# A fused attention, gated MLP and top-2 expert kernel: the second batch's attention in steps of three, the third chunk from the third unit on

## The chip, the cores and the metric

The kernel runs on one core of one Trainium2 chip. The metric is device time in microseconds of one execution. Before the change it was 981.42 us (median of 3 runs, 981.08 to 982.90).

## The reference, cut to what matters

```python
# attention: B=4 batches, H=8 heads, S=576 tokens, D=64, M=32 memory slots
a = exp(phi - max(phi, axis=tokens)); a /= sum(a, axis=tokens)
k_m, v_m = a^T @ k, a^T @ v                      # per head, 32 x 64
attn = softmax((q @ k_m^T) / 8); x = attn @ v_m  # x: 2304 tokens x 512
# gated MLP, d_ff = 1536
x = (sigmoid(x @ w_gate) * (x @ w_val)) @ w_out
# top-2 of 8 experts, F = 1024, noisy router
logits = x @ g + log1p(exp(x @ n)) * noise
out[t] = sum over the two best e of weight_e * (relu(x[t] @ w1[e]) @ w2[e])
```

## The kernel before

The weights of the gated MLP come as 64-bit numbers, and x and the weights are each kept as a high and a low fp16 part, so that every product is three passes of matmuls. The part that the change touches is the front of the program: attention, rounding of the weights, and the first products of the MLP, which all run at once.

**Products.** `stage1(c, (f,))` (lines 410 to 437) makes the gate and value of one chunk c of 256 tokens and one slice f of 128 hidden columns. It is called a product here: 24 matmuls of 256 columns on TensorE into one of four `pg` buffers of PSUM, then tanh on ScalarE (L432), a multiplication on VectorE (L433), and the split of the result into `gT` high (ScalarE, L435) and low (VectorE, L436), which frees the buffer. The third chunk (tokens 512 to 767) lies across two batches, so its products have 48 matmuls, of 64 and 192 columns, and need the attention of the second batch. The first three chunks have 36 products, and all of these are made before the second product of the MLP (`stage2`, L448) begins. Products are numbered 1 to 36 here, in the order in which TensorE has them.

**Weights.** `weights()` (lines 327 to 373) is a generator. A job is one matrix part of 256 columns (gate or value of a unit u, 6 units), or 256 rows of the output matrix, and each comes in two halves, loaded by `wload` into four `w64` buffers on the queue of SyncE. A half is converted by ScalarE (L321), two integer operations of VectorE (L323, L324) and an addition on GpSimd (L325, which frees the buffer). Per job ScalarE sums squares (L359); per unit a small matmul (`norm2`, L82, tile `pmx`) turns two sums into a scale, and then the pair is split (ScalarE L376, VectorE L377). A product of unit u needs the split pair u. Of the output matrix nothing is needed before L448.

**Attention.** `attend(b)` (line 953) is a generator too: softmax of the features (`features`, L201 to L206), the memories (`memory`, L163 to L190, for each half of the heads: two transposes, 20 or 40 small matmuls L176, the copies L178 and L181, a transpose L186, the copies L190 into `kbd`), a scale (`values_scale`, L213 and a `pmx` matmul), then for three groups of tokens the scores (L233, L230), their softmax over VectorE, ScalarE and GpSimd (L237 to L246), a transpose (L254) with its copy (L256), the result (L271, L264) and its split into the high and low x (ScalarE L274, VectorE L275). All of its PSUM tiles (`pa`) come from the same four `pg` buffers.

**What sets the order.** `build` (lines 966 to 1001) writes the front down as a mixture: `turns` takes one step of each generator named. After every product of the first two chunks come three steps of the weights and, while the second batch isn't done, one of the attention. The framework then orders each engine's instructions itself, by their priority and by what it expects to be ready; attention has a raised priority (`AHEAD1`). In the built program every engine works through its list strictly in this order, and so does the load queue on SyncE.

Of the kernel before, what the change touches and what calls it, by code (L numbers as in the profile page):

```python
# [61 lines left out]
class Kern:  # L62
# [841 lines left out]
    def build(self):  # L904
# [28 lines left out]
        def ahead_by(n):  # L933
            return tc.high_priority(n) if n else ExitStack()
# [26 lines left out]
        def attentions():  # L961
            for b in range(B):
                yield from attend(b)

        def turns(*gs):

            for g in gs:
                with ahead_by(offset.get(g, 0)):
                    next(g, None)
                while self.wanted:  # L970
                    self.att_load(*self.wanted.pop(0))

        self.attended = self.tokens_ready = 0
        atts, weights = attentions(), self.weights()
# [7 lines left out]
        def first(c, f):  # L982
            while self.tokens_ready < (c + 1) * CH:
                turns(atts)
            self.stage1(c, (f,))
        for u in range(6):
            while self.wdone < 2 * u + 2:
                turns(weights)
            for c in range(2):
                for f in (2 * u, 2 * u + 1):  # L990
                    first(c, f)
                    turns(weights, weights, weights)
                    if self.attended < 2:
                        turns(atts)
            if u >= 3:
                for _ in range(2):
                    first(*next(third))
                    turns(weights, weights, weights)
        for c, f in third:
            first(c, f)  # L1000
            turns(weights, weights, weights)
# [104 lines left out]
```

## Time and profile before

| what | value |
|---|---|
| median of 3 runs | 981.42 us |
| profiled execution | 978.12 us |
| its span (first to last instruction) | 976.4 us |
| TensorE busy | 922.5 us, 94% |
| VectorE, ScalarE busy | 468.7 us, 468.4 us, 48% each |
| mean granted TensorE clock | 0.973 |

The 1.72 us between the span and the time of the profiled execution lie around the program. The share of busy time is an average over the whole program: VectorE is below half over all, and near nine tenths in the front.

### The profile page before, as it was taken

The page shows a single profiled execution, that of the slowest core. Times are in us where ns is not written, and L with a number is a line of the kernel's source. Part 1 is how long each engine was busy: PE and PEld are TensorE (multiplying, and loading weights), DVE is VectorE, ACT ScalarE, POOL GpSimd, SP SyncE. Part 2 cuts the span into 40 slices and gives each one's busy share as a digit, 9 for nine tenths or more (in the row PEclk, how much of TensorE's full clock was granted, in tenths as well). Part 3 has the DMA queues.
Part 4 walks back from the last instruction along what each step waited for, and adds up shares of the span by engine and source line. Part 5 has one row for each costly group of instructions (what it writes and reads, how often), then busy time and mean ns, then how long its engine had stood idle before and what let it go on. Part 6 is the DMA issues. An engine that isn't in the chain of part 4 may idle for free.

```text
span 976.4 us, 18894 instructions
## 1 busy us (share of the span) xinstructions
PE 922.5 (94%) x7547; PEld 641.1 (66%) x7547; DVE 468.7 (48%) x1285; ACT 468.4 (48%) x979; POOL 209.6 (21%) x211
## 2 busy tenths in 40 slices
PE   5668889999999999999999989999999999999995
PEld 4447679766678877877776547657474757565652
DVE  3889884234543454567542504635353545432110
ACT  4788684234425344546431416647364646553230
POOL 1553420001011001020102154032232323131102
PEclk8689899999999999999999999999999999999998
DMA  9678474033022006474516959556757676745303
GB/s 301 219 221 284 148 248 154 18 89 104 23 71 72 23 23 189 133 216 147 202 24 168 350 112 195 179 129 130 200 118 204 115 187 122 172 80 75 40 12 43
DMA packets 125898, 135.28 MB, mean 139 GB/s; under 512 B 71792, under 2 KB 88304, under 8 KB 125296
## 3 DMA queue, kind: packets, MB, share of 16 engines
q1 hardware_dynamic: 115824, 113.30, 40.0%
q0 software_dynamic: 9984, 20.75, 11.9%
q8 instruction: 60, 0.98, 0.4%
q14 instruction: 30, 0.25, 0.1%
HBM read 87.97 MB, written 30.86 MB: 122 GB/s over the span
## 4 chain that ended last, share of the span: by engine, by line
PE 86%; DVE 4%; DMA 4%; ACT 2%; POOL 1%; issue 1%; SPq 0%; POOLq 0%; DVEq 0%; ACTq 0%
PE pg L426 26%; PE ph L770 20%; PE py L784 19%; PE px L448 14%; PE pa L233 1%; PE pa L176 1%; DMA w<-wo 1%; DVE pw L323 1%; DMA xe<-xg 1%; DMA w<-wv 1%; PE pa L271 1%; DVE w L377 1%; PE pl L476 1%; PE pmx L82 0%; DVE w L324 0%
## 5 line engine op out<-in xcount | busy, mean ns | idle before, releaser
L426 PE MATMUL pg<-x,w 128*128 128x256 f16 (+3 forms) x3456 | 309.1, 249 | 9.1 <-ACT w L376 4.8
L426 PEld LDWEIGHTS <-w 128*128 128x128 f16 x3456 | 271.2, 100 | 41.8 <-issue 7.0
L784 PEld LDWEIGHTS <-hT 128*128 128x128 f16 (+1 forms) x960 | 100.0, 105 | 105.5 <-DVE hT L776 1.0
L448 PE MATMUL px<-wo,gT 128*128 128x512 f16 x648 | 146.8, 379 | 0.0
L790 POOL DMA_INDIRECT out<-y,mts x40 | 63.9, 1596 | 227.4 <-ACT y L789 226.2
L770 PE MATMUL ph<-xe,w1a 128*128 128x312 f16 (+2 forms) x768 | 104.7, 299 | 4.3 <-DMA xe<-xg 4.3
L448 PEld LDWEIGHTS <-gT 128*128 128x128 f16 x648 | 62.2, 98 | 66.8
L784 PE MATMUL py<-w2a,hT 128*128 128x512 f16 (+1 forms) x480 | 104.9, 379 | 0.6 <-DVE hT L776 0.6
L784 PE MATMUL py<-w2b,hT 128*128 128x512 f16 (+1 forms) x480 | 104.7, 379 | 0.0
L770 PE MATMUL ph<-xe,w1b 128*128 128x312 f16 x768 | 102.8, 296 | 0.0
L432 ACT ACTIVATE sg<-pg,gs 128x256 f32<-128x256 f32 (+3 forms) x144 | 56.2, 416 | 90.2 <-PE pg L426 88.6
L592 POOL DMA_INDIRECT meta<-mt,vi x36 | 36.2, 1006 | 292.1 <-DVE vi L589 169.8
L776 DVE TENSOR_TENSOR hT<-r,hT 128x312 f16<-128x312 f32 (+2 forms) x128 | 56.6, 479 | 83.5 <-ACT hT L775 82.9
L770 PEld LDWEIGHTS <-w1a 128*128 128x128 f16 x768 | 75.6, 99 | 31.8 <-DMA xe<-xg 4.8
L770 PEld LDWEIGHTS <-w1b 128*128 128x128 f16 x768 | 75.2, 98 | 26.8
L789 ACT ACTIVATE y<-py,css 128x512 f32<-128x512 f32 (+1 forms) x40 | 27.5, 687 | 128.0 <-PE py L784 123.5
L433 DVE SCALAR_TENSOR_TENSOR pg<-sg,pg 128x256 f32<-128x256 f32 x108 | 45.9, 425 | 87.6 <-ACT sg L432 87.4
L774 ACT ACTIVATE r<-ph 128x312 f32<-128x312 f32 (+2 forms) x128 | 49.0, 428 | 78.8 <-PE ph L770 72.7
L435 ACT ACTIVATE gT<-pg 128x256 f16<-128x256 f32 x108 | 41.0, 380 | 46.0 <-DVE pg L433 45.7
L755 POOL DMA_INDIRECT xg<-xs,mts x40 | 44.9, 1122 | 72.6 <-DMA xe<-xg 27.8
L436 DVE SCALAR_TENSOR_TENSOR gT<-pg,gT 128x256 f16<-128x256 f32 x108 | 45.4, 420 | 27.9 <-ACT gT L435 27.9
L775 ACT CAST hT<-r 128x312 f16<-128x312 f32 (+2 forms) x128 | 52.4, 460 | 0.4
(307 smaller groups left out, 870.5 us busy)
## 6 DMA issues: line engine op xcount, KB each, us to landing
wo<-w SPq DMA_DIRECT2D x48, 512.0 KB, 5.6
st<-kv SPq DMA_DIRECT2D x16, 512.0 KB, 5.2
f<-w SPq DMA_DIRECT2D x16, 512.0 KB, 6.2
wsp<-hl SPq DMA_DIRECT2D x16, 512.0 KB, 3.5
w<-wg SPq DMA_DIRECT2D x12, 512.0 KB, 5.0
w<-wv SPq DMA_DIRECT2D x12, 512.0 KB, 4.9
w<-wo SPq DMA_DIRECT2D x12, 512.0 KB, 4.0
out<-z SPq DMA_DIRECT2D x23, 256.0 KB, 3.0
```

The lines of the kernel that those rows point to most:

```text
L426: nc.tensor.matmul(pg[:, j, s:e], w[:, l, k, fo : fo + P], self.xT[b][r][:, k, t0 : t0 + e - s], start=n == 0, stop=n == 3 * KT - 1)
L432: nc.scalar.activation(sg[:, s:e], pg[:, 0, s:e], AF.Tanh, scale=self.gate_scale(b, u))
L433: nc.vector.scalar_tensor_tensor(pg[:, 1, :], sg, 1.0, pg[:, 1, :], op0=ALU.add, op1=ALU.mult)
L436: nc.vector.scalar_tensor_tensor(g[:, 1, :], pg[:, 1, :], 2.0 ** -16, g[:, 0, :], op0=ALU.mult, op1=ALU.subtract)
L448: nc.tensor.matmul(p, g[:, l, t * P : (t + 1) * P], self.wob[f // 2][:, r, f % 2, :], start=f + i == 0, stop=f == FT - 1 and i == 2)
L755: self.nc.gpsimd.indirect_dma_start(out=xg.rearrange("p a b -> p (a b)"), out_offset=None, in_=self.xs[:rows, :], in_offset=bass.IndirectO ...
L770: nc.tensor.matmul(p[:, : t1 - t0], w1[:, l, k, f * P : (f + 1) * P], xe[:, x, t0:t1], start=n == 0, stop=n == 3 * KT - 1)
L774: nc.scalar.activation(r, p[:, : t1 - t0], AF.Relu, scale=2.0 ** -19)
L775: nc.scalar.copy(self.hT[:, 0, f, t0:t1], r)
L776: nc.vector.tensor_sub(self.hT[:, 1, f, t0:t1], r, self.hT[:, 0, f, t0:t1])
L784: nc.tensor.matmul(py, self.hT[:, l, f, i * P : i * P + m], w2[:, w, f, :], start=n == 0, stop=n == 3 * F2T - 1)
L790: d = nc.gpsimd.indirect_dma_start(out=self.out, out_offset=bass.IndirectOffsetOnAxis(ap=mt[:m, 0:1], axis=0), in_=y[:m], in_offset=None, ...
```

## The change

In the loop over the six units, attention takes up to three steps, not one, after each product of the first two chunks. The products of the third chunk start in the loop with the third unit (u = 2) instead of the fourth, three for each unit instead of two, so that all twelve are taken in the loop; beside each of these the weights take two steps instead of three. What is computed, and how many instructions there are, stays the same.

```diff
@@ -990,12 +990,13 @@
                 for f in (2 * u, 2 * u + 1):
                     first(c, f)
                     turns(weights, weights, weights)
-                    if self.attended < 2:
-                        turns(atts)
-            if u >= 3:
-                for _ in range(2):
+                    for _ in range(3):
+                        if self.attended < 2:
+                            turns(atts)
+            if u >= 2:
+                for _ in range(3):
                     first(*next(third))
-                    turns(weights, weights, weights)
+                    turns(weights, weights)
         for c, f in third:
             first(c, f)
             turns(weights, weights, weights)
```

On TensorE, this stands in the list before the change where the fourth product ends (`pg_658`) and the fifth, the first of the second unit (`w2`), begins (`pg_707`):

```order
L426 MATMUL pg_658<-x0_289,w1_82 128x256
L82 MATMUL pmx_471<-wum_428,onef_64 128x2
L426 LDWEIGHTS w2_83
L426 MATMUL pg_707<-x0_289,w2_83 128x256
L426 LDWEIGHTS w2_83
L426 MATMUL pg_707<-x1_290,w2_83 128x256
```

And this stands there after it, from the end of the fourth product (`pg_747`) to the fifth (`pg_824`); `pa_805` and `pa_872` are the scores of the second batch, `pmx_694` the scale of the fourth pair of weights, `pmx_797` the scale of the second batch:

```order
L426 MATMUL pg_747<-x0_289,w1_82 128x256
L82 MATMUL pmx_471<-wum_428,onef_64 128x2
L176 MATMUL pa_720<-st_554,a_710 32x128 x2
L186 MATMUL pa_789<-idf_60,km_741 128x128
L233 MATMUL pa_805<-kbd0_125,st_661 128x64 x8
L82 MATMUL pmx_694<-wum_538,onef_64 128x2
L426 LDWEIGHTS w2_83
L426 MATMUL pg_824<-x0_289,w2_83 128x256
L426 LDWEIGHTS w2_83
L426 MATMUL pg_824<-x1_290,w2_83 128x256
L82 MATMUL pmx_797<-vm_793,onef_64 128x1
```

The memories and the first scores of the second batch, and two scales, now come ahead of the fifth product. Before, the scores stood at the twelfth and thirteenth product, and attention ended inside the twentieth; now it ends inside the seventh. Products of the third chunk stood from the 17th place on and now stand from the 13th on.

On VectorE, this stands in the list before the change from the end of the fourth product (its `gT_686`) to the end of the fifth (`gT_737`):

```order
L436 SCALAR_TENSOR_TENSOR gT_686<-pg_658,gT_686 128x256
L88 TENSOR_SCALAR w3s_644<-w3h_643 128x2
L89 TENSOR_SCALAR w3i_645<-w3h_643 128x2
L433 SCALAR_TENSOR_TENSOR pg_707<-sg_732,pg_707 128x256
L324 SCALAR_TENSOR_TENSOR w10_91<-w64_545,pw_741 128x512
L323 TENSOR_SCALAR pw_748<-w64_593 128x512
L377 SCALAR_TENSOR_TENSOR w6_87<-w7_88,w3s_644,w6_87 128x1024
L436 SCALAR_TENSOR_TENSOR gT_737<-pg_707,gT_737 128x256
```

And after it the same place begins so (the fourth product is `pg_747`; `smx` and `ex` belong to the second batch's softmax):

```order
L436 SCALAR_TENSOR_TENSOR gT_775<-pg_747,gT_775 128x256
L324 SCALAR_TENSOR_TENSOR w9_90<-w64_461,pw_611 128x512
L201 TENSOR_REDUCE pmx_1051<-phi_905 128x1
L323 TENSOR_SCALAR pw_781<-w64_536 128x512
L323 TENSOR_SCALAR pw_858<-w64_545 128x512
L87 TENSOR_SCALAR sv1h_799<-pmx_797 128x1
L237 TENSOR_REDUCE smx_814<-pa_805 128x16
L88 TENSOR_SCALAR sv1s_800<-sv1h_799 128x1
L89 TENSOR_SCALAR sv1i_801<-sv1h_799 128x1
L239 TENSOR_TENSOR ex_816<-pa_805,smx_814 128x512
L237 TENSOR_REDUCE smx_881<-pa_872 128x16
```

The softmax of the second batch now stands between the fourth and the fifth product, 27 instructions where there were 6.

## Rows read from the trace of the kernel before

**Rows 1.** The page's busy tenths in 40 slices of 24.4 us.
```profile
PE   5668889999999999999999989999999999999995
DVE  3889884234543454567542504635353545432110
PEclk8689899999999999999999999999999999999998
```

**Rows 2.** Stretches: length, busy PE, PEld, DVE, ACT, POOL; clock, DMA share, GB/s.
```profile
39.20:62.60 23.40, 15.29 (x109) 12.26 (x110) 20.41 (x39) 17.50 (x29) 12.90 (x10) 0.79 0.79 250
62.70:92.40 29.70, 25.83 (x265) 20.68 (x264) 27.11 (x48) 25.80 (x62) 12.52 (x9) 0.93 0.83 262
92.40:137.00 44.60, 38.60 (x312) 30.51 (x313) 36.11 (x99) 31.59 (x63) 20.47 (x38) 0.85 0.55 175
137.00:182.10 45.10, 45.10 (x650) 43.20 (x649) 21.80 (x42) 22.31 (x52) 0.00 (x0) 1.00 0.45 152
```

**Rows 3.** Timeline of TensorE: start, length, what [idle before <-releaser].
```profile
16.72 1.46 PE L233 MATMUL pa<-kbd,x 128*128 128x64 f32 x12
...
39.16 0.60 PE L426 MATMUL pg<-x,w 128*128 128x256 f16 x2 [4.84 <-ACT w L376]
...
43.82 1.81 PE L264 MATMUL pa<-th,vbd 128*128 128x64 f32 x8
...
62.68 4.59 PE L426 MATMUL pg<-x,w 128*128 128x256 f16 x23 [2.77 <-DVE gT L436]
...
92.46 2.36 PE L233 MATMUL pa<-kbd,st 128*128 128x64 f32 x16 [1.48 <-DVE gT L436]
...
96.21 6.08 PE L426 MATMUL pg<-x,w 128*128 128x256 f16 x34
...
136.10 1.00 PE L264 MATMUL pa<-th,vbd 128*128 128x64 f32 x8
136.94 45.20 PE L426 MATMUL pg<-x,w 128*128 128x256 f16 x647
181.97 0.31 PE L82 MATMUL pmx<-wrm,onef 128*128 128x1 f32 x2
182.14 15.70 PE L448 MATMUL px<-wo,gT 128*128 128x512 f16 x72
```

**Rows 4.** Timeline of VectorE at the end of the nineteenth product.
```profile
140.72 0.41 DVE L436 SCALAR_TENSOR_TENSOR gT<-pg,gT 128x256 f16<-128x256 f32 x1
```

**Rows 5.** Timeline of ScalarE: the second batch's copies into kbd, first half of the heads.
```profile
75.34 0.41 ACT L190 COPY kbd<-pa 64x64 f32<-64x64 f32 x2
```

**Rows 6.** Groups on ScalarE, 20 to 137 us: busy us, mean ns | idle before, releasers.
```profile
L321 ACT ACTIVATE w<-w 128x512 int32<-128x512 uint32 x35 | 22.8, 666 | 5.3 <-DMA w<-wo 2.6 <-DMA w<-wg 2.5
...
L432 ACT ACTIVATE sg<-pg,gs 128x256 f32<-128x256 f32 x16 | 7.2, 463 | 2.6 <-PE pg L426 2.6
L435 ACT ACTIVATE gT<-pg 128x256 f16<-128x256 f32 x17 | 6.4, 374 | 0.4 <-DVE pg L433 0.3
...
L376 ACT ACTIVATE w<-w,w3s 128x1024 f16<-128x1024 f32 x2 | 2.3, 1142 | 0.0
...
L181 ACT COPY vbd<-pa 32x64 f32<-32x64 f32 x8 | 1.6, 201 | 0.1
L164 ACT COPY a<-pa 128x512 f32<-128x512 f32 x2 | 1.2, 586 | 1.2 <-PE pa L163 1.2
...
L213 ACT ACTIVATE x<-vbd 128x512 bf16<-128x512 f32 x1 | 0.6, 614 | 0.0
```

**Rows 7.** Waits of TensorE from 39 to 137 us: total, times, longest.
```profile
PE pmx L82 <- ACT w L359: 5.1, 2, 4.6
...
PE pg L426 <- DVE gT L436: 3.5, 3, 2.8
```

**Rows 8.** Waits of VectorE from 39 to 137 us, in the same form.
```profile
DVE pw L323 <- DMA w<-wv: 0.8, 2, 0.6
```

**Rows 9.** A stretch as in rows 2, by the granted clock.
```profile
94.00:100.70 6.70, 6.18 (x31) 4.68 (x30) 5.86 (x17) 4.40 (x9) 2.58 (x2) 0.50 0.58 175
```

## The prediction

> **What bounds the kernel now.** I read the page's slices first [rows 1]: TensorE is full nearly everywhere, and only the first six slices show it below nine tenths; there VectorE stands at eight and nine, and the granted clock is lowered. So the change, which touches only this front, is worth what it does to the moment at which TensorE leaves it. That is the first matmul of L448 at 182.14 us [rows 3]; from there on TensorE is busy to the end and the built order of the work is the old one, so an earlier or later L448 moves the end by as much.
>
> Second, the stretches [rows 2]. From 39.2 to 137 us TensorE is busy 15.3 + 25.8 + 38.6 = 79.7 of 97.7 us, partly at half clock, and VectorE 20.4 + 27.1 + 36.1 = 83.6. From 137 us on TensorE has no gap, and VectorE is idle for half of the time. So the front has two parts: one in which weights, attention and products wait for each other, and one in which a backlog of products runs off.
>
> Third, the timeline of TensorE [rows 3]. The backlog at 136.94 us is 647 matmuls in 45.20 us; a product of the third chunk has 48, and by the built order these are 17 products less one matmul: 45.20 / 17 = 2.66 us each, at a granted clock of 1.00, which is the 2.4 GHz level. The second batch's attention runs from its first scores at 92.46 to the end of its last result at 136.10 + 1.00 = 137.10: 44.6 us, with eight products in between. The first batch's took from 16.72 to 43.82 + 1.81 = 45.63: 28.9 us, with hardly a product between, and with a wait of 4.84 us for the first weights in it.
>
> **The change part by part.** *One step of attention becomes three.* It adds no instruction. It removes the second batch's attention from products 12 to 20 and puts it between the fourth product and the end of the seventh, on every engine. From the eighth product on TensorE then has a plain list: 29 products and two scales (0.3 us each, as the one at 181.97 [rows 3]). If none of them waits, L448 comes 29 x 2.66 + 0.6 = 77.7 us after the eighth product starts. Break-even is therefore a start of the eighth product at 182.1 - 77.7 = 104.4 us. Before, products 12 to 19 were still to come at 92.46 us, spread over 44.6 us.
>
> When does it start? The scores need the copies into kbd on ScalarE. Before, the first half's two copies ended at 75.34 + 0.41 = 75.75 us [rows 5]. Ahead of the end of the second half's copies in the changed list stands what stood ahead of that place, plus the second half of `memory` and the sum for the batch's scale, less some weights and products. Added are the copies L164 (0.59), L167 and L178 (about 0.25 each, taken like the smallest copies), four L181 (0.80), two L190 (0.40) and L213 (0.61 and its read of 0.2): 3.1 us. Gone are two L321 (1.33), one L376 (1.14), two L432 (0.93) and one L435 (0.37): 3.8 us [rows 6]. With the same idle time the scores can start at 75.75 - 0.7, about 75.1. The price: the fifth product, which began at 62.68 [rows 3], now stands behind them in TensorE's list and begins near 77; TensorE has only attention from the end of the fourth product on, some 12 us.
>
> From the scores to the end of attention I take bounds from the two rows that there are. Low: the first batch's 28.9 us. High: the second batch's 44.6 less the five products of 2.66 us that are no longer inside (eight before, three now): 31.3. I take 28.9, since three products in it fill no more than the waits that the first batch had for its first weights and for its chain. Eighth product: 75.1 + 28.9 = 104.0. L448: 104.0 + 77.7 = 181.7 us, that is 0.4 us earlier.
>
> A second sum, from VectorE, ends close to it. Up to the end of the nineteenth product (L436 at 140.72 + 0.41 = 141.1 us [rows 4]) the same instructions stand in VectorE's list before and after, in another order; its work is thus the same 83.6 us from 39 us on, and what can change is the 14.1 us that it idles. With the same idle time the nineteenth product is again released at 141.1. There are four buffers, so the 23rd product may start then at the latest, and L448 comes no earlier than 141.1 + 14 x 2.66 = 178.3. That bounds the gain at 3.8 us, unless VectorE's idle time shrinks as well.
>
> *The third chunk from the third unit on.* Its products go from the 17th place to the 13th. They need no new weights, so they are cover for TensorE while the later pairs are made; and that is already in the plain list assumed above. It costs nothing: an L436 of the third chunk is as long as any other. *Two steps of weights beside them.* The same steps, written later; the splits of the output matrix stay more than 30 us ahead of L448. Taken as 0.
>
> *Loads.* SyncE's queue now has the second batch's q, and the third batch's two phi and two kv loads, ahead of halves of the last pair of weights. The third batch's four are 1.8 MB, or 6.8 us at the 262 GB/s of that stretch [rows 2]. VectorE waited for value weights only 0.8 us in two waits [rows 8], and the sixth unit's products are six of the last seven, yet the conversions of these halves stand ahead of the sixth and seventh product on ScalarE. Bounds 0 and 6.8 us; I take 0, to which the row of waits is nearer. *A scale inside a product.* The sixth pair's scale now stands inside the eleventh product on TensorE. Such a scale waited up to 4.6 us before, 5.1 us in two waits [rows 7]. Bounds 0 and 4.6; I take 0, because TensorE is then ahead of VectorE in filled buffers, and what it loses it would have waited for one of them.
>
> Sum against the profiled execution: 978.12 - 0.4 = 977.7 us. The median of the runs shown is 981.42, 3.30 us above that execution (its span 976.4 and 1.72 around it), so the forecast is 981.42 - 0.4 = 981.0 us. About 0.2%, or 2.0 us, is what a measurement of this kernel can tell from no change.
>
> **The rivals.** *Faster: the compact chain.* The first batch's 28.9 us hold 4.84 us in which TensorE waited for the first weights [rows 3]; the second batch's need not, since its units' weights are further on. The eighth product then starts at 104.0 - 4.8 = 99.2, and TensorE could be out at 176.9; VectorE's sum lets it out at 178.3. Gain 3.8 us: 977.6 us. For it: four buffers stay free for products once attention is over, where before results waited for buffers (3.5 us on L436 [rows 7]). Against it: VectorE would have to keep up with 2.66 us per product at once.
>
> *Slower: the low clock in the thin stretch.* Between the fourth and the eighth product TensorE now has little work with waits between. Before, a wait for a buffer and the second batch's scores were followed by a stretch at a granted clock of 0.50, the 1.2 GHz level [rows 9], and 34 matmuls took 6.08 us in it [rows 3], 0.179 us each against 2.66 / 24 = 0.111. If products five to seven run so, they take 3 x 24 x (0.179 - 0.111) = 4.9 us more: eighth product at 108.9, L448 at 186.6, time 981.42 + 4.5 = 985.9 us. It decides from a start of the eighth product at 106.4 on (2.0 us past break-even). For it: TensorE stands nearly still from about 62 to 75 us. Against it: the first batch's 28.9 us already contain low clock. The Trainium skill (TensorE: Matmul & The Clock Gate, section A second HAM failure mode: psum-queue depth-cycling) says that short idle gaps between groups of matmuls can make the clock swing between its two levels; by that rule this rival's 985.9 us are the sum, without it 981.0. The trace agrees that the clock fell to 0.50 around the scores at 92.46 us.
>
> *Later weights.* VectorE has 27 instructions between the fourth and the fifth product where it had 6, and the fourth pair's splits are among them. A late pair is covered until the 16th product, the first that needs it, by the third chunk's products 13 to 15. If the cover is gone, a wait of the longest kind seen, 4.84 us [rows 3], stands there: 985.8 us. I hold it for little.
>
> **How the numbers follow.** No change to be seen (within 2.0 us): 0.38. Faster by the compact chain: 0.33. Slower: 0.29 (low clock 0.19, late weights, loads or scale 0.10). The likeliest gives 981.0, with its own range 979.4 to 983.4. The range for 8 in 10 reaches to the faster case with some of VectorE's idle time saved as well (3.8 + 3.0 us) and to the low clock with part of the loads' 6.8 us (4.5 + 2.1): 974.6 to 988.0.
>
> **What would show it.** Right: scores of the second batch near 75 us, fifth product near 77, eighth product between 102 and 106, no gap of TensorE over 1 us after it, and the nineteenth L436 near 141. The faster rival shows an eighth product before 102; the slower one a granted clock of 0.50 through most of 62 to 100 us and the eighth product after 106. The forecast is wrong in its steps if TensorE waits after the eighth product for a pair of weights (L377), a load or the sixth pair's scale, or if L448 moves and the end doesn't.

## The result and the profile after

The changed kernel is slower: 994.9 us median of 4 runs (989.3 to 999.0) against 982.0 of the kernel before on the same chip, ratio 1.0113 [1.0081, 1.0145]. Run again on another chip it gave 1.0116 [1.0075, 1.0157] (e13_change below). The forecast was 981.0 us with a range of 974.6 to 988.0: time, sign and range are missed. The profiled execution took 992.82 us with a span of 991.0 (before 978.12 and 976.4).

The slices of the page, as in [rows 1]; one is 24.8 us:

```profile
PE   6558979999999999999999989999999999999996
DVE  2876875324554355467643423735354544443110
PEclk9985989999999999999999999999999999999998
```

What differs lies in the first six slices: TensorE's second and third are at 5 where they were at 6, its sixth (124 to 149 us) at 7 where it was at 8, and VectorE has no nine any more. The loss is in the front again; from L448 on the two spans agree within 2 us (784.0 us from its first matmul to TensorE's last one before, 785.8 after). TensorE's timeline shows where, to be held against [rows 3]:

```profile
28.95 1.11 PE L254 MATMUL pa<-idf,ex 128*128 128x128 f32 x4 [4.00 <-POOL ex L246]
...
73.75 0.64 PE L176 MATMUL pa<-st,a 64*32 64x128 f32 x4 [9.00 <-DMA st<-kv]
...
75.51 3.52 PE L233 MATMUL pa<-kbd,st 128*128 128x64 f32 x16
...
106.61 1.10 PE L264 MATMUL pa<-th,vbd 128*128 128x64 f32 x8
...
119.29 0.38 PE L82 MATMUL pmx<-wum,onef 128*128 128x2 f32 x2 [1.07 <-ACT w L359]
119.53 19.99 PE L426 MATMUL pg<-x,w 128*128 128x256 f16 x252
146.13 0.58 PE L82 MATMUL pmx<-wom,onef 128*128 128x1 f32 x2 [6.60 <-DVE wom L366]
146.57 48.68 PE L426 MATMUL pg<-x,w 128*128 128x256 f16 x639
195.09 0.31 PE L82 MATMUL pmx<-wrm,onef 128*128 128x1 f32 x2
195.26 2.10 PE L448 MATMUL px<-wo,gT 128*128 128x512 f16 x9
```

L448 begins at 195.26 us instead of 182.14. The first line is a mark for what chance adds: that wait for the first batch's softmax, ahead of all that the change moves in this stretch, ended at 26.50 us in the trace before, and at 26.5 in e1_att3, whose list is the changed one up to there. In e7_bwom and e15_before_w4, where that part is the kernel before's, it ended at 29.1 and 28.7. So 2.4 of the 13.1 us are not the change's, and below I count from that mark. The largest new wait is the one of 9.00 us for a load of keys and values. But the forecast had TensorE without products there, and from the mark the eighth product begins only 1.5 us later than forecast (the table further down). The largest that the forecast had no room for is the wait of 6.60 us: TensorE stands inside the 19th product at a small sum of 0.58 us, which adds up the sums of the output weights over the partitions (`norm2`, tile `wom`), because VectorE has not made `wom`. In the kernel before the same sum stood inside the 19th product too and waited 0.3 us. The mark and this sum in the trace before:

```profile
26.50 1.11 PE L254 MATMUL pa<-idf,ex 128*128 128x128 f32 x4 [4.00 <-POOL ex L246]
...
133.46 0.38 PE L82 MATMUL pmx<-wom,onef 128*128 128x1 f32 x2 [0.34 <-DVE wom L366]
```

The stretches, with the columns of [rows 2], cut at the eighth product's start, at that wait and at the end of the half clock:

```profile
64.40:107.90 43.50, 30.18 (x150) 20.97 (x151) 29.21 (x62) 26.61 (x55) 16.44 (x12) 0.61 0.63 184
107.90:139.50 31.60, 30.53 (x350) 27.76 (x348) 27.21 (x55) 24.99 (x50) 15.47 (x12) 1.00 0.61 195
139.50:146.10 6.60, 0.03 (x1) 0.00 (x0) 5.70 (x17) 4.57 (x10) 5.20 (x15) 0.80 0.01 4
146.10:150.30 4.20, 4.17 (x28) 3.24 (x29) 3.48 (x18) 2.64 (x6) 1.12 (x13) 0.50 0.92 320
150.30:195.20 44.90, 44.90 (x620) 42.72 (x618) 20.14 (x39) 20.93 (x48) 0.00 (x0) 1.00 0.45 151
```

The third row is the wait. The fourth is its echo: the granted clock is 0.50 (1.2 GHz) for the first 4.2 us in which TensorE works again, 28 matmuls where the next row has 58 in the same time. That costs some 2 us.

Why is `wom` late? Three views of the stretch in which the attention is now compact. VectorE first (start, length, idle before and its releaser):

```profile
76.20 0.69 DVE L323 TENSOR_SCALAR pw<-w 128x512 int32<-128x512 int32 x1 [0.64 <-DMA w<-wv]
80.06 0.16 DVE L87 TENSOR_SCALAR sv1h<-pmx 128x1 int32<-128x1 int32 x1 [3.16 <-PE pmx L82]
80.13 0.68 DVE L237 TENSOR_REDUCE smx<-pa 128x16 f32<-128x512 f32 x1
...
83.60 0.69 DVE L237 TENSOR_REDUCE smx<-pa 128x16 f32<-128x512 f32 x1 [2.06 <-PE pa L233]
...
85.81 0.68 DVE L324 SCALAR_TENSOR_TENSOR w<-w,pw 128x512 int32<-128x512 int32 x1
```

L323 and L324 are the two steps of a conversion on VectorE. Nine microseconds lie between the last first step here and the next second step, because the batch's scale, the scores and the softmax stand between them in VectorE's list and wait for TensorE. GpSimd, which finishes each conversion (L325), is idle behind them:

```profile
70.05 4.70 POOL L325 TENSOR_TENSOR w<-w,w 128x512 int32<-128x512 int32 x3 [0.77 <-ACT w L321]
86.62 1.28 POOL L325 TENSOR_TENSOR w<-w,w 128x512 int32<-128x512 int32 x1 [11.87 <-ACT ex L240]
```

And L325 frees the buffer that SyncE's next weight load needs:

```profile
74.78 0.37 SPq L310 DMA_DIRECT2D w<-wg  x1
...
87.93 0.38 SPq L310 DMA_DIRECT2D w<-wg  x1
...
92.18 6.48 SPq L310 DMA_DIRECT2D w<-wv  x2
```

For 13 us no weights are asked for. Of the 36 conversions 25 were done by 100 us before, 20 after; the output weights' sums are ready at 133.4 us before, 146.1 after (10.3 us later from the mark).

### The profile page after: what moved, and what is told of

The parts are those of the page before. It is cut to its first block, busy times and chain, and to the rows that moved or that the text cites. A ratio compares the mean times of both kernels' runs of the same rounds, so it can differ in the third digit from the quotient of the medians.

```text
span 991.0 us, 18900 instructions
## 1 busy us (share of the span) xinstructions
PE 930.9 (94%) x7547; PEld 646.5 (65%) x7547; DVE 466.0 (47%) x1285; ACT 469.0 (47%) x979; POOL 212.0 (21%) x211
## 4 chain that ended last, share of the span: by engine, by line
PE 81%; DMA 6%; DVE 5%; ACT 4%; issue 2%; POOL 1%; SPq 0%; POOLq 0%; DVEq 0%; ACTq 0%
PE pg L426 25%; PE py L784 18%; PE ph L770 17%; PE px L448 14%; DMA wo<-w 2%; PE pa L233 1%; PE pa L271 1%; DMA w<-wo 1%; DMA xe<-xg 1%; PE pa L176 1%; DVE pw L323 1%; DMA xg<-xs,mts 1%; ACT w L359 1%; PE pa L254 1%; PE pl L476 1%
## 5 line engine op out<-in xcount | busy, mean ns | idle before, releaser
L448 PE MATMUL px<-wo,gT 128*128 128x512 f16 x648 | 146.8, 379 | 0.0
L448 PEld LDWEIGHTS <-gT 128*128 128x128 f16 x648 | 62.2, 98 | 66.9
L776 DVE TENSOR_TENSOR hT<-r,hT 128x312 f16<-128x312 f32 (+2 forms) x128 | 56.6, 478 | 82.4 <-ACT hT L775 81.7
L436 DVE SCALAR_TENSOR_TENSOR gT<-pg,gT 128x256 f16<-128x256 f32 x108 | 45.5, 421 | 26.6 <-ACT gT L435 26.5
```

Of the source, the lines that this page charges most:

```text
L436: nc.vector.scalar_tensor_tensor(g[:, 1, :], pg[:, 1, :], 2.0 ** -16, g[:, 0, :], op0=ALU.mult, op1=ALU.subtract)
L448: nc.tensor.matmul(p, g[:, l, t * P : (t + 1) * P], self.wob[f // 2][:, r, f % 2, :], start=f + i == 0, stop=f == FT - 1 and i == 2)
L776: nc.vector.tensor_sub(self.hT[:, 1, f, t0:t1], r, self.hT[:, 0, f, t0:t1])
```

## The experiments

Each kernel was timed beside the kernel before on the same chip. The chips differ (medians of before: 984.3, 990.8, 984.3 and 983.2 us for the four groups), so only ratios are compared. A trace is one execution; from L448 on it takes 794 us (the kernel before, e13_change) to 807 us (e4_tail), and all four traces of the chip of e4_tail take 804 or more. So traces are compared by L448, counted from the mark. In 15 of the 16 traces its shift against the kernel before agrees with the timed ratio within 2.6 us; e16_change_w4 is the exception. Theory T: the loss is the scale's wait and the half clock behind it, and the output weights are late because three steps of attention in a row hold the conversions up.

### Which part of the change

e1_att3, the attention part alone:

```diff
-            if u >= 2:
-                for _ in range(3):
+            if u >= 3:
+                for _ in range(2):
                     first(*next(third))
-                    turns(weights, weights)
+                    turns(weights, weights, weights)
```

> Only the first part of the change: three steps of the attention beside each first product; the third chunk follows from the fourth unit on, two products and three turns of the weights each, as before. Theory T (the loss is TensorE's wait for the scale of the output weights, which stands inside the 19th product, 6.6 us in the changed kernel, and the half clock after it, some 4 us; the output weights are late because the attention's steps, taken closer together, hold the conversions of the weights up): the wait stays, 4 to 8 us, and the time is 988 to 998, like the whole change. Rival R1 (the thinner stretch of the first eight products, its chain of 32 us and its half clock, costs the time itself): 988 to 998 too. Rival R2 (the third chunk begun a unit earlier brings TensorE to the 19th product's scale too soon, and the conversions get two turns instead of three): the wait is under 2 us, 980 to 985.

Measured 1.0099 [1.0065, 1.0132]; the wait for the scale is 5.1 us.

e2_third, the other part alone:

```diff
-                    for _ in range(3):
-                        if self.attended < 2:
-                            turns(atts)
+                    if self.attended < 2:
+                        turns(atts)
```

> Only the second part: the third chunk follows from the third unit on, three products each with two turns of the weights; one step of the attention beside each first product, as before. T and R1: no wait over 1 us for the scale of the output weights, which is still inside the 19th product, 980 to 984, no difference to the kernel before. R2: the wait is there, 4 us or more, 988 to 996.

Measured 1.0007 [0.9984, 1.0029], with a wait of 1.6 us for the scale, a little over T's bound. R2 falls: the attention part is the whole loss, the third chunk's earlier place costs nothing that can be told.

e6_att2, two steps (`range(2)` in the place of `range(3)`):

> The whole change with two steps of the attention beside each first product instead of three: the second batch's scores come inside the 6th and 7th product (changed kernel: 4th and 5th; before: 12th and 13th), the attention's end inside the 10th. T: the conversions are held up less, so the wait for the scale of the output weights is shorter, 0 to 4 us, and the time 980 to 988. R1: the thin stretch is about two products longer than at three steps but no stall is taken away, 985 to 992. R2: 988 to 996, as the third chunk is as in the change.

Measured 1.0053 [1.0031, 1.0075], half the loss. But the wait is 5.3 us, not the 0 to 4 that T expected: from the mark the output weights are ready 5.3 us earlier than in the change, and TensorE is at the scale 4.0 us earlier as well. What counts at such a place is the difference of the two.

### The barrier and what is late

e3_wom18, the scale 18 turns later:

```diff
-        s, self.cinv = yield from self.norm2(cp, m, "wo")
+        s, self.cinv = yield from self.norm2(cp, m, "wo", 18)
```

> The whole change, but the matmul that adds up the scale of the output weights is taken 18 turns later: on TensorE it stands inside the 24th product instead of the 19th, some 13 us of products later. T: the wait of 6.6 us and the half clock behind it go, nothing else takes their place, and the time falls by 8 to 11 us to 982 to 986; the plain list of products ends at about 184 to 185 us (before 182.1). R1: the stretch up to the eighth product keeps the loss, 990 to 996. R3 (the output weights' lateness is passed on to the second products, whose weights are split behind that scale on VectorE and ScalarE): a wait of 3 us or more stands before the second products, and 987 to 993.

Measured 1.0032 [1.0013, 1.0052], 8 us under the change, the low end of what T said; L448 comes at 188.99 us, 186.5 with the mark of the trace before, where T had 184 to 185. TensorE's timeline:

```profile
119.60 0.38 PE L82 MATMUL pmx<-wum,onef 128*128 128x2 f32 x2 [1.53 <-ACT w L359]
...
142.21 2.84 PE L426 MATMUL pg<-x,w 128*128 128x64 f16 x48 [0.74 <-DVE gT L436]
...
146.28 10.76 PE L426 MATMUL pg<-x,w 128*128 128x64 f16 x144 [1.23 <-DVE gT L436]
156.88 0.28 PE L82 MATMUL pmx<-wom,onef 128*128 128x1 f32 x2
157.02 31.96 PE L426 MATMUL pg<-x,w 128*128 128x256 f16 x432
188.99 8.36 PE L448 MATMUL px<-wo,gT 128*128 128x512 f16 x38
```

The scale has no wait, though the weights are as late as ever (ready at 147.2 us); no half clock follows, and the waits behind its old place are of at most 1.23 us, so R3 falls. The thin stretch is the same as in the change, so R1 is worth at most the 3 us that are left; the list of products still holds 3.5 us of small waits.

e7_bwom, the control: the same edit in the kernel before.

> Control: the kernel before, with only the output weights' scale 18 turns later (inside the 22nd product instead of the 19th). T: the kernel before waits 0.3 us there, so nothing is gained: within 1.5 us of the kernel before. If a later scale is worth something by itself (the matmul or the conversions behind it in the way of the products), it is 3 us or more faster, and then what e3_wom18 gave back is not the stall alone.

Measured 0.9984 [0.9951, 1.0017]. A later scale is worth nothing that can be told where nothing waits for it.

e4_tail, the 9.00 us wait of the timeline: the last 64 rows of the keys and values stand in SyncE's queue behind weight loads that wait for GpSimd.

```diff
-                nc.sync.dma_start(t[:SH, SC, :], rows[SC * P :, cols])
+                (nc.gpsimd if b and g else nc.sync).dma_start(t[:SH, SC, :], rows[SC * P :, cols])
```

> The whole change, but the 64-row tails of the last two key-and-value loads of the second batch (and of the third) are issued by GpSimd instead of SyncE, so that they do not stand behind weight loads that wait for a buffer. The scale of the output weights stands inside the 20th product (changed kernel: the 19th). Theory T1a (the late tail, for which TensorE waits 9.0 us, is what makes the rest late, the output weights too): the wait of 9.0 us is under 2, the scores begin 6 to 8 us earlier, the wait for the output weights' scale falls under 2 us, and the time is 0 to 4 us over the kernel before. Theory T1b (the output weights are late because their conversions stand behind the attention's softmax on VectorE, wherever that begins): the scores begin earlier, yet the wait for the output weights' scale stays within 4 to 8 us, and the time is 6 to 12 us over the kernel before.

Measured 1.0052 [1.0016, 1.0088]. Its timeline:

```profile
63.34 1.90 PE L233 MATMUL pa<-kbd,st 128*128 128x64 f32 x16
...
79.64 0.59 PE L82 MATMUL pmx<-wum,onef 128*128 128x2 f32 x2 [5.16 <-ACT w L359]
...
140.49 0.58 PE L82 MATMUL pmx<-wom,onef 128*128 128x1 f32 x2 [5.14 <-DVE wom L366]
```

The scores come 12 us earlier and the time falls by about 6 us, yet the scale waits 5.1 us, as T1b said; the time, 5 us over the kernel before, lies between T1a's 0 to 4 and T1b's 6 to 12. The tail is a loss of its own, and part of the cause of the late weights: from the mark they are ready 5.8 us earlier than in the change, though still 4.4 later than before. The wait stays because TensorE is at the scale 4.3 us earlier too. Nor do all of the 12 us come back: 9 reach the eighth product, and a pair's scale now waits 5.16 us for its weights.

e5_w160, the later scale, and the weights' turns at the attention's priority:

```diff
-        offset[atts] = AHEAD1
+        offset[atts] = AHEAD1; offset[weights] = 160
```

> The whole change with the output weights' scale 18 turns later (as in e3_wom18, which was 3.2 us over the kernel before), and with the turns of the weights given the same priority as the attention's steps, so that VectorE, ScalarE and the queue of loads take the conversions before the attention's instructions where both wait. The output weights' scale then stands inside the 21st product. T1b: the output weights are ready some 8 to 12 us earlier than in e3_wom18 (there about 146), no wait of over 1 us for the scale though it stands three products earlier, and the time is within 3 us of e3_wom18. Rival T1a (the loads of keys and values are late, nothing else): the readiness of the output weights moves by less than 3 us, and the wait for the scale is 2 us or more, since it stands 8 us earlier. Rival R1 (the thin stretch costs the rest): the attention is later with the conversions ahead of it, the second batch's scores start at 78 or later, and the time is 3 us or more over e3_wom18.

Measured 1.0069 [1.0034, 1.0103]. TensorE's waits from 39 to 195 us (total, times, longest):

```profile
PE pmx L82 <- ACT w L359: 8.5, 3, 4.9
PE pa L254 <- POOL ex L246: 6.1, 1, 6.1
PE pa L176 <- DMA st<-kv: 5.1, 1, 5.1
```

Both sides are seen. The output weights are ready at 138.9 us, 8.3 earlier than in e3_wom18, though the tail is still waited for and the scores come later: the place of the conversions in the lists was enough to make them late. But now the softmax waits for GpSimd behind conversions, the scores begin at 78.9, the attention ends 6 us later, and the time is 3.6 us over e3_wom18, R1's outcome. Priority here only chose which of the two is late.

### Towards a kernel that beats both

e8_tail_wom, the edits of e3_wom18 and e4_tail together:

> Both: the early tails of e4_tail and the later scale of e3_wom18 in the changed kernel. T with T1a: 3 to 6 us faster than e3_wom18, so 0 to 3 us under the kernel before; the eighth product begins 6 to 8 us earlier than in the change. T with T1b: the sixth pair's scale (11th product) then waits 4 to 7 us for its weights in place of the keys and values, and the time is within 2 us of e3_wom18.

Measured 0.9992 [0.9960, 1.0023]: the loss is gone, 4 us under e3_wom18 (the intervals overlap), as T with T1a expected, and the eighth product begins 8 us earlier than in the change. Two pairs' scales wait 5.2 and 2.9 us.

e9_w40, on top of it `offset[weights] = 40`:

> e8_tail_wom (early tails, later output scale; as fast as the kernel before within 0.3%) with the turns of the weights 40 places of priority ahead, a quarter of what e5_w160 had. The fourth pair's scale waited 5.2 us and the sixth pair's 2.9 us there. If the conversions' place on VectorE sets these waits, they fall to 3 and 1 us or less, and the time is 2 to 4 us under e8_tail_wom, that is 2 to 5 us under the kernel before. If VectorE and GpSimd are simply full in this stretch, the attention loses what the weights gain (as in e5_w160, where the second batch's scores began 3 us later and GpSimd was waited for 6.1 us): within 1.5 us of e8_tail_wom.

Measured 0.9995 [0.9962, 1.0027], no change: the second answer. The waits for pairs' scales did fall, from 8.4 us in all to 3.5, but TensorE now waits 5.0 us for the softmax on VectorE (L244) and 5.4 us for L436, 2.1 in e8_tail_wom.

e10_att2, e8_tail_wom with two steps:

> e8_tail_wom with two steps of the attention beside each first product instead of three. If fewer steps leave the conversions more of VectorE, the output weights are ready 5 us or more earlier than in e8_tail_wom (139.4) and the pairs' scales wait less, and the time is 1 to 3 us under it. If the compact chain is worth its place, the time is 1 to 3 us over it, as the attention ends some 5 us later.

Measured 0.9970 [0.9946, 0.9994]. It leans to the first answer, but the intervals overlap, and the output weights are ready at 137.8 us, only 1.6 earlier. Inconclusive.

e12_w4, e8_tail_wom with the pairs' scales later:

```diff
-WAIT_W, WAIT_SPLIT, WAIT_TURN, WAIT_ROUTE = 2, 4, 5, 4
+WAIT_W, WAIT_SPLIT, WAIT_TURN, WAIT_ROUTE = 4, 4, 5, 4
```

> e8_tail_wom with every scale of a pair of weights taken four turns after its sums instead of two: the fifth pair's scale stands inside the 9th product instead of the 7th, the sixth pair's inside the 14th instead of the 11th, the output weights' inside the 28th. If the barrier in TensorE's order is what these waits are, whoever is late, the waits of 2.9 and 5.2 us shrink to under 1 and under 4 us, and the time is 1 to 4 us under e8_tail_wom. If the products behind need those weights at once, the wait moves from the scale to the first product of the pair (on ScalarE's or VectorE's split), and the time is within 1.5 us of e8_tail_wom.

Measured 0.9947 [0.9923, 0.9972], faster than both kernels and 4.5 us under e8_tail_wom, though these two intervals just overlap. Its timeline:

```profile
60.78 2.00 PE L233 MATMUL pa<-kbd,st 128*128 128x64 f32 x16 [0.19 <-ACT vbd L181]
...
84.06 0.59 PE L82 MATMUL pmx<-wum,onef 128*128 128x2 f32 x2
...
114.49 0.31 PE L82 MATMUL pmx<-wum,onef 128*128 128x2 f32 x2
...
156.75 0.31 PE L82 MATMUL pmx<-wom,onef 128*128 128x1 f32 x2
178.28 15.70 PE L448 MATMUL px<-wo,gT 128*128 128x512 f16 x72
```

The scales from the scores on have no wait, and L448 begins at 178.28 although this execution reached the mark 2.1 us later than before.

e13_change, the changed kernel again:

> The changed kernel itself, unchanged, on the chip of these three: theory T: again 8 to 13 us over the kernel before, with the wait of 5 to 8 us for the output weights' scale and a stretch of half clock behind it. If the first comparison (four runs spread over 10 us) was an accident of that chip, it is under 5 us.

Measured 1.0116 [1.0075, 1.0157]; the wait is 7.1 us, half clock behind it. The first comparison was no accident.

e14_att2_w4, e12_w4 with two steps:

> e12_w4 (early tails, later scales of the pairs and of the output weights; 0.53% under the kernel before) with two steps of the attention beside each first product. If conversions on VectorE still bound the stretch, two steps gain 1 to 3 us more on e12_w4; if the scales were the only barriers, it is within 1.5 us of it.

Measured 0.9944 [0.9918, 0.9969]: the same as e12_w4.

e15_before_w4, the kernel before with both later scales:

> The kernel before (one step, third chunk from the fourth unit on) with the same later scales of the pairs and of the output weights. If the change together with early tails has a gain of its own, this stays within 2 us of the kernel before and e12_w4 remains 3 us or more faster. If the later scales alone are the gain, it is 3 to 6 us under the kernel before, too, as its wait of 4.6 us for a pair's scale goes.

Measured 0.9966 [0.9943, 0.9989]. Most of the gain of e12_w4 is the later scales', with or without the change. It does not come as expected, though: the wait for a pair's scale grew to 6.7 us, and L448 came 2.6 us earlier from the mark all the same. What went are TensorE's waits for VectorE's L436 and L275, 8.3 us from 39 us on in the trace before and 0.9 here; why they went was not tried. That the compact attention adds the other 2 us is likely but not shown; the intervals overlap.

e16_change_w4, the change with both later scales and the late tails:

> The changed kernel with the later scales of the pairs and of the output weights, the tails late as in the change. If the barriers of the scales are the whole loss: 1 to 5 us under e3_wom18, so within 2 us of the kernel before. If the late tail and the thin stretch are the rest: within 1 us of e3_wom18, 2 to 5 us over the kernel before.

Measured 1.0035 [1.0009, 1.0060], as e3_wom18. By the times the rest of the loss is thus the late tail: moving it gave 4 us (e3_wom18 to e8_tail_wom), 6 (change to e4_tail) and 9 (here to e12_w4, where the intervals are far apart). Its one profile fits badly: L448 at 181.8 us, from the mark 0.8 earlier than before where the times say 3.4 later, and the waits for the tail 4.4 us in two. That stays open.

## Why the prediction was wrong

The table counts from the mark (the end of that 4.00 us wait of the first batch). The list is what TensorE has from the eighth product's first matmul up to L448; its waits are the gaps of over 0.06 us in it.

| | mark, us | eighth product | list | its waits | list without waits | L448 |
|---|---|---|---|---|---|---|
| prediction | 26.5 | 77.5 | 77.7 | 0 | 77.7 | 155.2 |
| kernel before | 26.5 | | | | | 155.6 |
| change | 28.9 | 79.0 | 87.3 | 7.7 | 79.7 | 166.3 |
| e3_wom18 | 29.0 | 78.7 | 81.2 | 3.5 | 77.7 | 160.0 |
| e4_tail | 29.1 | 69.8 | 88.4 | 7.2 | 81.2 | 158.2 |
| e8_tail_wom | 26.7 | 70.5 | 83.0 | 5.0 | 78.0 | 153.5 |
| e12_w4 | 28.6 | 67.3 | 82.4 | 4.5 | 77.9 | 149.7 |

- **The failed step** is "If none of them waits, L448 comes 29 x 2.66 + 0.6 = 77.7 us after the eighth product starts". The products were sized rightly: without its waits the list took 77.7 to 78.0 us where no half clock fell into it (e3_wom18, e8_tail_wom, e12_w4). But it has three scales where the prediction counts two of 0.3 us each, and that of the output weights waited 6.60 us, with 2.0 us of half clock behind, and the sixth pair's 1.07. That is 9.7 of the 10.7 us by which L448 comes later than before. The prediction had priced the wait of the sixth pair's scale (0 to 4.6) and never that of the output weights', which it did not move.
- *Two steps of weights*, "written later ... Taken as 0": the splits do have over 30 us of room (the last ends at 163.9 us), but what TensorE meets first is the scale, which it reaches at 139.5. The third chunk's part is rightly 0 (e2_third).
- *Later weights*, "I hold it for little": it was this rival, for the output weights instead of a pair. What it says, that VectorE has 27 instructions between the fourth and the fifth product, fits what e5_w160 shows, and the late tail held those instructions up further (e4_tail). Its cover by the third chunk's products was the error: a product covers a late pair, but no scale that stands ahead of it in the list.
- *The eighth product*: scores at 75.51 against "about 75.1", the fifth product at 79.2 against 77, the chain 32.2 us against 28.9, just over its upper bound of 31.3. From the mark it began 1.5 us later than forecast and 1.1 after break-even. The scores' time was right by luck: a DMA set it, not ScalarE's work. With the tail out of the way they began at 63.34 us (e4_tail), some 14 us earlier from the mark than the sum by ScalarE's list with the old idle time allowed.
- *Loads*, taken as 0 of 0 to 6.8 us: the third batch's loads did no harm that is seen, but the tail of the second batch's own, not looked for, kept TensorE waiting 9.00 us. Without it the eighth product came 9 us earlier (e4_tail), more than the 4.8 that the faster rival hoped for, but the time was still over the kernel before, since the scale waited on.
- *VectorE's sum*, "the nineteenth product is again released at 141.1": it was released at 153.9. The idle time is what changed. From 39 to 137 us, the stretch of [rows 2], VectorE had idled 14 us; from 41.4 (as far from the mark) to 146.0, where TensorE's wait ends, it idled 25.7: busy 78.9 of 104.6 us. Steps taken in a row wait for one another; that spread out, as before, their waits were filled with conversions is my reading of the two lists and was not tried by itself.
- *The low clock in the thin stretch* came much as that rival drew it, 0.61 on the mean from 64.4 to 107.9 us, with the eighth product past its point of 106.4 in that trace, but only by the 2.4 us of chance. Its price was not measured by itself: e3_wom18, with the same stretch and no wait at the scale, is still 3 us over the kernel before.

## What to carry over

A small matmul that sums a scale is a barrier in TensorE's list: before a change that moves work between engines, ask of each such matmul when its input will be ready and when TensorE will be there, also of those that the change doesn't move. Steps of a dependent chain that were put side by side in an in-order list made the queues behind them wait, down to the loads. And a scale placed later, well ahead of its use, cost nothing that could be told (e7_bwom) and gave back 0.8% where TensorE stood at it (the change to e3_wom18). With all scales later and the tail moved, the changed order is 0.5% faster than the kernel before; the later scales alone give that kernel 0.3%.

## What the runs showed of the hardware

After the gap of 5.1 to 7.1 us at the scale the granted clock was 0.50 for the next 3 to 5 us of work in all five profiles that had it (the change twice, e1_att3, e4_tail, e6_att2), and in e3_wom18, e8_tail_wom and e12_w4, without it, 1.00 from the eighth product to L448. Here the stretch behind the gap in e6_att2, and e8_tail_wom from the end of the attention to L448, columns as above:

```profile
136.50:141.20 4.70, 4.70 (x33) 3.79 (x34) 3.91 (x19) 3.35 (x7) 0.97 (x11) 0.50 0.95 329
```

```profile
97.40:180.20 82.80, 77.78 (x991) 72.12 (x989) 58.16 (x130) 53.46 (x112) 21.87 (x38) 1.00 0.55 182
```

So these waits of TensorE cost more than their length: in the change 6.6 us cost some 8.6. The gaps of up to 2.9 us in the second row did not lower the clock, nor did one of 3.1 us in e16_change_w4, though gaps of 2.5 us in e14_att2_w4 and 2.9 us in e9_w40 were followed by half clock. The rule that the prediction cites from the Trainium skill (TensorE: Matmul & The Clock Gate, section A second HAM failure mode: psum-queue depth-cycling) speaks of short gaps between groups of matmuls; the case here that cost time was one long gap.
